# Four of the tiles that TensorE transposes go by DMA transfers of their own

## The chip, the cores and the metric

The kernel runs on one core of one Trainium2 chip. The metric is the time of one execution on the device in microseconds (us); the median of the runs is compared. TensorE multiplies matrices into PSUM, VectorE and ScalarE work element by element, GpSimd (POOL) does small things, and SyncE issues most DMA transfers, in order, from one queue.

## The reference

One block of a transformer with adaptive layer normalization. x has 2048 rows of 640; there are 32 heads of 128, with keys and values given (2048 each). In short:

```python
mod = (_silu(c) @ w_mod).reshape(c.shape[0], 6, 1, -1)
h = _layernorm(x, axis=-1) * (1 + ca) + sa
q = (h @ wq) per head
scores = jnp.einsum('bhqd,bhkd->bhqk', q, k_cache) * Dh ** (-0.5)
p = _softmax(scores, axis=-1)
o = jnp.einsum('bhqk,bhkd->bhqd', p, v_cache)
x = x + ga * (o @ wo)
h = _layernorm(x, axis=-1) * (1 + cb) + sb
x = x + gb * _B_ref(h, B_w1, B_w2, B_w3, B_w4)
```

`_B_ref` is a mixer with shifted rows and an MLP of width 1728. The change touches attention alone: the scores of 128 queries of one head against 2048 keys become exponentials, and these have to be turned (keys on the partitions) before they can be multiplied by V.

## The kernel before

**Tiles and steps.** A tile is 128 queries of one head: 16 tiles a head, 512 in all (NG), numbered through. The main loop (L684) takes one tile a step. In step s:

- TensorE makes the scores of tile s into the four banks of Sps, in two halves (`qk`, L352; its instructions stand at L359 and L15). Behind each half it multiplies half of the turned exponentials of tile s - 10 by V (`pv`, L365 and L373; PVD = 10). Then come pieces of the next head's Q (`q_piece`, L301) or a quarter of a transpose (below).
- VectorE reads each half of the scores, writes it scaled and negated to negS, and gathers the minimum of each row (L723). negS has three buffers, so tile s waits for the exponential of tile s - 3.
- POOL joins the two minima (L728). ScalarE takes the exponential into one place of `ring` (L731), 128 x 2048 bf16. It also copies the results of P V out of PSUM (L708), Q (L308), and TensorE's transposes (L333).

**Turning the exponentials.** `ring` has 20 places. Of 32 tiles (a pair of heads) 27 are turned by DMA, in trios of neighbouring tiles: when the last of the three has its exponential, SyncE issues one transfer from three neighbouring places to three others (`transpose`, L284, L286). The other five (tiles 3, 10, 17, 24 and 31 of the pair, the table PE_T) are turned by TensorE: eight f32 transposes of 128 x 128 (two bf16 keys taken as one f32), in four quarters spread over the half steps of two steps (`t_piece`, L319, L326), starting at the step that the table names (four steps after the tile, six for the last of the five). ScalarE copies the two halves back into the same place (`t_evac`, L330, L333). For such a tile VectorE writes even and odd keys apart (L720 to L722), and `pv` reads every second column (L372).

**Places.** The order of places is planned before the loop, L236 to L279. Trios use six windows of three places (WIN), tiles for TensorE the two single places 6 and 19 (ONE) in turn. PSL is the place that a tile's exponentials are written to, TSL that of the turned ones; `take` gives the place that has been free longest.

**Waits.** A recording layer (`Prog`) notes what each operation reads and writes, and puts a semaphore wait wherever another engine's or a transfer's work has to be over. All engines work in the order in which the loop records. SyncE's queue holds, besides the transposes, the loads of K (L222, by DMA transpose as well), of V (L231) and of wq (L226), one each for each head; K at the head's third step, V at its eleventh.

The pieces of Q are placed by `PIECES` (L335), in half steps that the table of TensorE's transposes leaves free. After the 512 tiles the output projection, the mixer and the MLP follow (from 1208 us).

Of the kernel before, what the change touches and what calls it, by code (L numbers as in the profile page):

```python
# [123 lines left out]
def bass_adaLN_cond__mha_block_cached__mixer_s_mlp__prompt_kernel(  # L124
# [21 lines left out]
    with ExitStack() as es:  # L146
# [9 lines left out]
        if True:  # L156
            with ExitStack() as es1:
# [4 lines left out]
                PE_AT = {32 * i + t: 32 * i + a for i in range(NG // 32) for t, a in PE_T.items()}  # L162
                PE_AT[NG - 2], PE_AT[NG - 1] = NG + 1, NG + 3
                del PE_AT[NG - 8]
                US = KT * (SQ + 4)
                small = sb1("small", [128, 4 * NQT + 32], F32)
                ring = sb1("ring", [128, NS, SK], BF16)
# [3 lines left out]
                mod_bc = sb1("mod_bc", [128, 4 * D], F32)  # L171
                hTx = sb1("hTx", [128, US], BF16)
                Of = sb1("Of", [128, 4, 2, 130], F32)
# [50 lines left out]
                def load_wq(h):  # L224
                    hb = h % 2
                    G.dma("sync", lambda e: e.dma_start(wq[:, hb], A_wq[:, h * 128:(h + 1) * 128].rearrange("(k p) d -> p k d", p=128)),  # L226
                          ("wq", hb), w=[("wq", hb)])
# [6 lines left out]
                is_pe = lambda g: g in PE_AT  # L234

                WIN = [0, 3, 7, 10, 13, 16]  # L236
                ONE = [6, 19]
                PSL, TSL, first_of, last_of = {}, {}, {}, {}
                free_at = dict(zip(WIN, (0, 2, 108, 1, 105, 106)))
                free_at.update(zip(ONE, (0, 1)))  # L240

                def take(opts):
                    a = min((a for a in opts if free_at[a] is not None), key=lambda a: free_at[a])
                    free_at[a] = None
                    return a
                todo = []
                for g in range(NG):
                    if is_pe(g):
                        PSL[g] = TSL[g] = g
                    else:  # L250
                        todo.append(g)
                trios = []
                while todo:
# [6 lines left out]
                for s in range(NG):  # L260
                    end = s >= NG - 10
                    g = s - PVD
                    if g in PSL and is_pe(g):
                        free_at[TSL[g]] = 100 + s
                    elif g in last_of:
                        free_at[TSL[last_of[g][0]]] = 100 + s + 1
                    if is_pe(s):
                        PSL[s] = TSL[s] = take(ONE)
                    if s in first_of:
                        m = first_of[s]  # L270
                        a = take([13] if m is trios[-1] else WIN[0:3] if end else WIN)
                        for i, g in enumerate(m):
                            PSL[g] = a + i
                    if s in last_of:
                        m = last_of[s]
                        a = take([7] if m is trios[-1] else WIN[3:6] if end else WIN)
                        for i, g in enumerate(m):
                            TSL[g] = a + i
                        free_at[PSL[m[0]]] = 100 + s + 6.5  # L279
# [4 lines left out]
                def transpose(m):  # L284
                    a, b, n = PSL[m[0]], TSL[m[0]], len(m)
                    G.dma("sync", lambda e: e.dma_start_transpose(  # L286
                        PTs[:, b:b + n].rearrange("p r k q -> p (r k) q"), ring[:, a:a + n].rearrange("p r s -> p (r s)")),
                        ("t", b), r=[k for i in range(n) for k in slot(a + i)], w=[k for i in range(n) for k in slot(b + i)])
# [395 lines left out]
                for s in range(NG + PVD + LAG):  # L684
                    h, j = divmod(s, NQT)
                    g_ = s - PVD
                    evacs = []
                    for half in range(2):
                        if s == 1:
                            spin_j(4 - half)  # L690
                        if s < NG:
                            qk(s, half)
                        if 0 <= g_ < NG:
                            pv(g_, half)
                        if h + 1 < H and 2 * s + half in PIECES[h]:
                            cc, q = PIECES[h][2 * s + half]
                            q_piece(h + 1, cc, q)
                            if q == KT - 1:
                                evacs.append((q_evac, h + 1, cc))
                        for g, r in t_of(s):  # L700
                            t_piece(g, r, half)
                            if half == 1:
                                evacs.append((t_evac, g, r))
                        for fn, *args in TAIL.get((s, half), ()):
                            fn(*args)
                    if 0 <= g_ < NG and g_ % 2 == 1:
                        p = g_ // 2
                        G.op("scalar", lambda a, p=p: a.copy(  # L708
                            Of[:, p % 4].rearrange("p z d -> p (z d)")[:, 0:259], PO[:, (p % 2) * 512:(p % 2) * 512 + 259]),
                            r=[("O", p % 2)], w=[("Of", p % 4)])  # L710
                    for fn, x, y in evacs:
                        fn(x, y)
                    for fn, *args in EARLY.get(s, ()):
                        fn(*args)
                    for half in range(2):
                        if s < NG:
                            r8 = s % 8
                            dst = negS[:, s % 3, half * 1024:(half + 1) * 1024]
                            src = Sps[:, half * 1024:(half + 1) * 1024]
                            if is_pe(s):  # L720
                                dst = dst.rearrange("p (b i z) -> p b z i", b=4, z=2)
                                src = src.rearrange("p (b z i) -> p b z i", b=4, z=2)  # L722
                            G.op("vector", lambda v, half=half, dst=dst, src=src, r8=r8: v.tensor_scalar(  # L723
                                out=dst, in0=src, scalar1=-SCALE, scalar2=None, op0=ALU.mult, op1=ALU.min,
                                accum_out=(nm0 if half == 0 else nm1)[:, r8:r8 + 1]),
                                r=[("S", half)], w=[("negS", s % 3), ("nmh", half, r8)])
                    if s < NG:
                        G.op("gpsimd", lambda g, r8=r8: g.tensor_scalar(  # L728
                            out=nm[:, r8:r8 + 1], in0=nm0[:, r8:r8 + 1], scalar1=nm1[:, r8:r8 + 1], scalar2=None, op0=ALU.min),
                            r=[("nmh", 0, r8), ("nmh", 1, r8)], w=[("nm", r8)])  # L730
                        G.op("scalar", lambda a, s=s, r8=r8: a.activation(  # L731
                            ring[:, PSL[s], :], negS[:, s % 3, :], ACT.Exp, bias=nm[:, r8:r8 + 1], scale=-1.0),
                            r=[("negS", s % 3), ("nm", r8)], w=slot(PSL[s]))
                        for fn, *args in LATE.get(s, ()):
                            fn(*args)
                        if s == OTS[0]:
                            ot0(0)
                        if s == 9 and H > 1:
                            load_k(1)
                            if H > 2:  # L740
                                load_wq(2)
                        if s in last_of:
                            transpose(last_of[s])
                        if j == 2 and h >= 1 and h + 1 < H:
                            load_k(h + 1)
                        if s in OTS[1:]:
                            ot0(OTS.index(s, 1))
                        if h and j == (0, 3)[h % 2] and h + 2 < H:
                            load_wq(h + 2)
                        if j == PVD and h + 1 < H:  # L750
                            load_v(h + 1)
                    if 0 <= s - PVD - LAG:
                        gr, z = divmod(s - PVD - LAG, 4)
                        if z == 0:
                            rcp(gr)
                        norm(gr, z)
                    if s == NG + PVD - 9:
                        G.op("gpsimd", lambda g: g.memset(mhalf, -0.5), w=["mhalf"] + NEG)
                        ot0(3)
                        load_ot(1, 0, H // 2, 0)  # L760
                        load_ot(1, H // 2, H, 1)
                        load_xt(0, 1)
# [281 lines left out]
```

## Time and profile before

| | |
|---|---|
| median of three runs | 1525.32 us (1523.91 to 1526.04) |
| the profiled execution | 1523.88 us, span 1522.0 us |
| attention, first to last VectorE instruction of L723 | 19.1 to 1207.6 us |
| transposes by DMA (L286) | 144, median 6.48 us in SyncE's queue, 9.6 us to landing |
| K loads (L222) | 32, median 2.3 us in the queue, 5.1 us to landing |
| copies of TensorE's transposes (L333) | 160 |
| TensorE's granted clock | 0.999 |

In the rows of groups the first number after the bar is busy time, then the mean length of one instruction in ns, then the engine's idle time before them and what ended it. Neighbouring instructions of VectorE and of ScalarE overlap in the records (the next begins before the last has ended), so the distance of two starts, not the length, is what an instruction costs. A SyncE row starts when the transfer's waits are over and ends when the queue goes on to the next entry; the landing comes later.

### The profile page before, as it was taken

The page shows a single profiled execution, that of the slowest core. Times are in us where ns is not written, and L with a number is a line of the kernel's source. Part 1 is how long each engine was busy: PE and PEld are TensorE (multiplying, and loading weights), DVE is VectorE, ACT ScalarE, POOL GpSimd, SP SyncE. Part 2 cuts the span into 40 slices and gives each one's busy share as a digit, 9 for nine tenths or more (in the row PEclk, how much of TensorE's full clock was granted, in tenths as well). Part 3 has the DMA queues.
Part 4 walks back from the last instruction along what each step waited for, and adds up shares of the span by engine and source line. Part 5 has one row for each costly group of instructions (what it writes and reads, how often), then busy time and mean ns, then how long its engine had stood idle before and what let it go on. Part 6 is the DMA issues. An engine that isn't in the chain of part 4 may idle for free.

```text
span 1522.0 us, 32831 instructions
## 1 busy us (share of the span) xinstructions
PE 1495.4 (98%) x13757; PEld 922.7 (61%) x12733; DVE 1369.4 (90%) x2424; ACT 1256.8 (83%) x1182; POOL 629.1 (41%) x1404
## 2 busy tenths in 40 slices
PE   8999999999999999999999999999999999999999
PEld 4566666656666666666666666666666665554545
DVE  8999999999999999999999999999999746767425
ACT  6999999999999999999999999999999700034230
POOL 1244444444444444444444444444444433333100
PEclk9999999999999999999999999999999999999999
DMA  9999999999999999999999999999999999734101
GB/s 325 254 244 247 251 229 255 234 229 249 243 229 254 243 243 232 242 244 241 240 236 241 245 233 247 243 234 246 246 240 229 242 222 215 152 83 108 35 22 35
DMA packets 1155297, 330.30 MB, mean 217 GB/s; under 512 B 1133322, under 2 KB 1149770, under 8 KB 1155146
## 3 DMA queue, kind: packets, MB, share of 16 engines
q1 hardware_dynamic: 1146656, 307.09, 100.5%
q0 software_dynamic: 6144, 16.79, 3.4%
q10 hardware_dynamic: 2346, 4.34, 0.8%
q8 instruction: 104, 1.70, 0.5%
q14 instruction: 47, 0.39, 0.1%
HBM read 43.48 MB, written 19.40 MB: 41 GB/s over the span
## 4 chain that ended last, share of the span: by engine, by line
ACT 73%; PE 18%; DVE 4%; DMA 2%; SPq 1%; issue 1%; POOL 0%; DVEq 0%; POOLq 0%
ACT ring L731 60%; PE Sps L654 7%; ACT ring L333 5%; ACT Of L708 4%; ACT kv L308 4%; PE Sps L981 4%; DVE negS L723 3%; PE Oaug L932 2%; PE QPp L932 2%; PE Sps L917 1%; DMA ring<-ring 1%; SPq L622 1%; SPq L286 1%; DMA ring<-in_A_x_dram 1%; ACT hTx L487 1%
## 5 line engine op out<-in xcount | busy, mean ns | idle before, releaser
L723 DVE TENSOR_SCALAR_CACHE_REDUCE negS<-Sps 128x1024 f32<-128x1024 f32 x1024 | 1174.6, 1225 | 5.8 <-PE Sps L15 3.0
L731 ACT ACTIVATE ring<-negS,small 128x2048 bf16<-128x2048 f32 x512 | 1115.5, 2403 | 1.6 <-POOL small L728 1.1
L373 PEld LDWEIGHTS PTp<-kv,ring 128*128 128x128 bf16 x8192 | 557.9, 98 | 302.7 <-issue 86.9
L373 PE MATMUL PTp<-kv,ring 128*128 128x129 bf16 x8192 | 645.1, 220 | 5.5 <-DMA ring<-ring 5.1
L359 PE MATMUL Sps<-kv 128*128 128x512 bf16 x1024 | 394.4, 385 | 8.1 <-DVE negS L723 4.5
L728 POOL TENSOR_SCALAR small<-small 128x1 f32<-128x1 f32 x512 | 146.1, 285 | 597.0 <-DVE negS L723 596.9
L15 PE MATMUL Sps<-kv 128*128 128x512 bf16 x1024 | 387.9, 379 | 0.0
L708 ACT COPY Of<-PTp 128x259 f32<-128x259 f32 x256 | 194.6, 760 | 3.9 <-PE PTp L373 3.9
L573 POOL TENSOR_SCALAR On<-Of,small 128x128 bf16<-128x128 f32 x512 | 189.8, 371 | 13.0
L359 PEld LDWEIGHTS Sps<-kv 128*128 128x128 bf16 x1024 | 98.2, 96 | 124.1 <-DVE negS L723 82.7
L566 POOL TENSOR_TENSOR small<-Of,small 128x4 f32<-128x4 f32 x128 | 133.1, 1040 | 13.7 <-ACT Of L708 13.4
L301 PE MATMUL QPp<-hTx,kv 128*128 128x512 bf16 x325 | 121.2, 378 | 1.1 <-ACT kv L308 1.1
L301 PE MATMUL Oaug<-hTx,kv 128*128 128x512 bf16 x315 | 118.5, 378 | 3.0 <-ACT kv L308 1.3
L580 POOL DMA_DIRECT2D o_scratch<-On x128 | 103.8, 811 | 40.8 <-POOL On L573 37.2
L723 DVE DVE_READ_ACCUMULATOR negS<-Sps 128x1 f32 x1024 | 90.5, 88 | 0.0
L855 ACT ACT_TABLE_LOAD x1 | 1.3, 1283 | 105.3 <-POOL hTx L873 105.3
L333 ACT COPY ring<-Oaug 128x512 f32<-128x512 f32 x78 | 76.6, 982 | 0.0
L333 ACT COPY ring<-QPp 128x512 f32<-128x512 f32 x77 | 76.3, 992 | 0.0
L767 POOL TENSOR_SCALAR negS<-negS 128x1 f32<-128x1 f32 x48 | 24.4, 509 | 116.8 <-DVE negS L776 116.8
L654 PE MATMUL Sps<-wo,negS 128*128 128x128 bf16 (+1 forms) x512 | 71.5, 299 | 0.4 <-DVE ring L782 0.4
L985 DVE TENSOR_TENSOR ring<-Sps,ring 128x640 f32<-128x640 f32 x15 | 12.4, 825 | 60.8 <-PE Sps L981 60.8
L308 ACT CAST kv<-QPp 128x512 bf16<-128x512 f32 x65 | 62.2, 956 | 1.3 <-PE QPp L301 1.3
(118 smaller groups left out, 1091.6 us busy)
## 6 DMA issues: line engine op xcount, KB each, us to landing
kv<-in_A_v_cache_dram SPq DMA_DIRECT2D x32, 512.0 KB, 5.3
o_scratch<-On POOLq DMA_DIRECT2D x128, 128.0 KB, 5.0
ring<-in_A_x_dram SPq DMA_DIRECT2D x8, 640.0 KB, 4.9
kv<-in_A_wq_dram SPq DMA_DIRECT2D x32, 160.0 KB, 3.6
wo<-in_A_wo_dram SPq DMA_DIRECT2D x1, 5120.0 KB, 21.6
ring<-in_w_mod_dram SPq DMA_DIRECT2D x5, 640.0 KB, 8.6
out_dram<-wo SPq DMA_DIRECT2D x15, 160.0 KB, 1.8
ring<-ring SPq DMA_TRANSPOSE x144, 9.6
```

Of the source, the lines that this page charges most:

```text
L15: return t.add_instruction(mybir.InstMatmult(name=t.bass.get_next_instruction_name(), ins=[t.lower_ap(rhs), t.lower_ap(lhsT)], outs=[t.low ...
L301: G.op("tensor", lambda t: t.matmul(JB[jb], wq[:, hb, q, :], hT[:, q, cc * 512:(cc + 1) * 512], start=(q == 0), stop=(q == KT - 1)), r=[(" ...
L333: G.op("scalar", lambda a: a.copy(dst, src), r=keys[-1:], w=[("PT", TSL[g], r)])
L359: ins = (t.matmul if c2 == 0 else partial(same_weights, t))(Sps[:, col:col + 512], QT[:, hb, j * 128:(j + 1) * 128], KTs[:, hb, col:col + ...
L373: ins = t.matmul(ob[:, 0:129], pt, Vaug[:, hb, kt, 0:129], start=(kt == 0), stop=(kt == NKT - 1))
L566: G.op("gpsimd", lambda g: g.tensor_tensor(out=rl[:, 4 * b:4 * b + 4], in0=Of[:].rearrange("p a z d -> p (a z) d")[:, 4 * b:4 * b + 4, 128 ...
L573: G.op("gpsimd", lambda g: g.tensor_scalar(out=On[:, b, z, :], in0=Of[:, 2 * b + z // 2, z % 2, 0:128], scalar1=rl[:, 4 * b + z:4 * b + z ...
L654: ins = t.matmul(YB[b][:, c0:c0 + cw], OTj[pr % 2][:, 2 * hh + z, :], wo[:, hh, c0:c0 + cw], start=(hh == 0), stop=(hh == H - 1))
L708: G.op("scalar", lambda a, p=p: a.copy(Of[:, p % 4].rearrange("p z d -> p (z d)")[:, 0:259], PO[:, (p % 2) * 512:(p % 2) * 512 + 259]), r= ...
L723: G.op("vector", lambda v, half=half, dst=dst, src=src, r8=r8: v.tensor_scalar(out=dst, in0=src, scalar1=-SCALE, scalar2=None, op0=ALU.mul ...
L728: G.op("gpsimd", lambda g, r8=r8: g.tensor_scalar(out=nm[:, r8:r8 + 1], in0=nm0[:, r8:r8 + 1], scalar1=nm1[:, r8:r8 + 1], scalar2=None, op ...
L731: G.op("scalar", lambda a, s=s, r8=r8: a.activation(ring[:, PSL[s], :], negS[:, s % 3, :], ACT.Exp, bias=nm[:, r8:r8 + 1], scale=-1.0), r= ...
```

## The change

In the second, sixth, tenth and fourteenth pair of heads the second of the five tiles (tiles 42, 170, 298 and 426, the list LONE) is no longer turned by TensorE. Its exponentials go to a single place as before; three steps later SyncE issues a transfer of this tile alone to the other single place, ahead of the trio that ends in the same step. The source's place is given back to the plan at that step, the target's when P V of the tile is over. VectorE and `pv` treat the tile like one of a trio, because `is_pe` is false for it. The four quarters on TensorE and the two copies on ScalarE fall away for it. `PIECES` is still made from the table (the tiles are taken out of PE_AT ahead of it, and the pieces of Q stand in the same half steps as before).

```diff
                 del PE_AT[NG - 8]
+                LONE = [32 * i + 10 for i in (1, 5, 9, 13)]
+                for g in LONE:
+                    del PE_AT[g]
...
                     if is_pe(g):
                         PSL[g] = TSL[g] = g
-                    else:
+                    elif g not in LONE:
                         todo.append(g)
...
                     g = s - PVD
-                    if g in PSL and is_pe(g):
+                    if g in PSL and (is_pe(g) or g in LONE):
                         free_at[TSL[g]] = 100 + s
                     elif g in last_of:
                         free_at[TSL[last_of[g][0]]] = 100 + s + 1
-                    if is_pe(s):
+                    if is_pe(s) or s in LONE:
                         PSL[s] = TSL[s] = take(ONE)
+                    if s - 3 in LONE:
+                        TSL[s - 3] = take(ONE)
+                        free_at[PSL[s - 3]] = 100 + s
...
+                        if s - 3 in LONE:
+                            transpose([s - 3])
                         if s in last_of:
                             transpose(last_of[s])
```

## The prediction

> **What bounds the kernel now.** I read the page first, then the list of waits, then VectorE and ScalarE in order of time, last SyncE's queue at the four places that the change touches. In the page:
>
> ```profile
> PE 1495.4 (98%) x13757; PEld 922.7 (61%) x12733; DVE 1369.4 (90%) x2424; ACT 1256.8 (83%) x1182; POOL 629.1 (41%) x1404
> ACT 73%; PE 18%; DVE 4%; DMA 2%; SPq 1%; issue 1%; POOL 0%; DVEq 0%; POOLq 0%
> L723 DVE TENSOR_SCALAR_CACHE_REDUCE negS<-Sps 128x1024 f32<-128x1024 f32 x1024 | 1174.6, 1225 | 5.8 <-PE Sps L15 3.0
> L731 ACT ACTIVATE ring<-negS,small 128x2048 bf16<-128x2048 f32 x512 | 1115.5, 2403 | 1.6 <-POOL small L728 1.1
> ```
>
> The attention stage (19 to 1208 us) holds the change. TensorE looks fullest, but is not the limit: its weight loads wait 82.7 us in all for VectorE (L723), while VectorE is idle only 5.8 us before L723. VectorE's 1,024 halves follow each other in 1.145 us, so 32 tiles (a pair of heads) need 64 x 1.145 = 73.28 us. ScalarE is idle even less, and the chain of waits runs through it (73%). So two engines are full at almost the same rate. Where they meet, around tile 255 (VectorE, then ScalarE in order of time, then the chain of waits in order of time):
>
> ```profile
> 616.48 1.22 DVE L723 TENSOR_SCALAR_CACHE_REDUCE negS<-Sps 128x1024 f32<-128x1024 f32 x1
> 618.21 1.23 DVE L723 TENSOR_SCALAR_CACHE_REDUCE negS<-Sps 128x1024 f32<-128x1024 f32 x1 [0.50 <-ACT ring L731]
> ```
>
> ```profile
> 615.06 4.56 ACT L731 ACTIVATE ring<-negS,small 128x2048 bf16<-128x2048 f32 x2
> 618.86 1.03 ACT L708 COPY Of<-PTp 128x259 f32<-128x259 f32 x1
> ```
>
> ```profile
> 606.26 3.79 ACT ring L731 x2
> 610.05 0.26 ACT Of L708
> 610.32 0.49 ACT kv L308
> 612.71 0.47 ACT ring L333
> 615.35 0.49 ACT ring L333
> ```
>
> VectorE starts 1.73 us after its last start instead of 1.145: it waits for an exponential of three tiles earlier, since negS has three buffers. ScalarE's cost by those rows, for 32 tiles: 32 exponentials x 1.895 + 16 copies of O x 0.26 + 8 of Q and 10 of transposed halves x 0.48 = 60.6 + 4.2 + 8.6 = 73.4 us, 0.16 more than VectorE needs. I went through the starts of all L723 instructions and added what exceeds 1.145 us. After a tile with ScalarE as releaser, or with ScalarE as the last one busy: tiles 127, 241, 255, 273, 280, 287, 305, 319, 337, 351, 383, 433, 447, 465, 479 and 497 give 0.27, 0.11, 0.58, 0.16, 0.02, 0.21, 0.16, 0.23, 0.15, 0.23, 0.58, 0.14, 0.23, 0.16, 0.23 and 0.16: 3.6 us. After one with TensorE late: 0.35, 1.15 and 0.41 (tiles 21, 28, 38), 1.17 (134), 0.15 (358), 0.07 (387) and 0.4 at the end: 3.7 us. Nothing else holds this stage up after tile 20, so a lighter ScalarE can give back at most 3.6 us.
>
> **The change, part by part.** For tiles 42, 170, 298 and 426:
>
> *Taken from ScalarE*: two copies (L333) a tile, 0.47 + 0.49 = 0.96 us, 3.8 us in all, at the 4th and 5th step after the tile. This lies on the path wherever ScalarE is the one behind. Over four pairs ScalarE runs 4 x 0.16 = 0.64 us over VectorE's time; one removal of 0.96 us covers that. Not all can be banked: the exponentials of tiles 288 to 319 start 1.1 to 2.2 us after VectorE's end of the same tile, and the least such distance anywhere is 0.42 us, so a lead of at least 1.1 - 0.4 = 0.7 us is won there, enough for four pairs. In the other three places the distance is partly at its least already (0.42 us in tiles 128 to 191), and some is lost. Bounds: all 3.6 us, or only the waits in the 22 tiles after tiles 298 and 426 (0.16 + 0.23 + 0.14 + 0.23 = 0.8 us). I take 3.1: 0.16 a pair says that the balance itself turns, which is nearer to the upper end; 0.5 us stays at local peaks.
>
> *Taken from TensorE*: 8 f32 transposes a tile with their loads (L326, 273 ns each, overlapped; the half steps that hold them last 1.13 us in TensorE's order). It isn't late there, so 0; the place in the order stays empty, since the pieces of Q stay where they were.
>
> *VectorE and POOL*: the tile's minimum is written without the even-odd split. Medians are 1.221 us with the split and 1.220 us without: 0. POOL: nothing moves. P V of the tile reads plain columns instead of every second one: same shape, 0.
>
> *Added to SyncE's queue*: one transfer (L286's function) a tile of 128 x 2048, three steps after the tile, after V's load and ahead of the trio that ends in that step. It has to wait for the exponential, three steps old, and for P V of the tile seven before, whose place it writes. The queue at the four places (SyncE in order of time):
>
> ```profile
> 135.90 0.58 SPq L231 DMA_DIRECT2D kv<-in_A_v_cache_dram  x1
> 138.27 7.32 SPq L286 DMA_TRANSPOSE ring<-ring  x1
> 430.95 0.58 SPq L231 DMA_DIRECT2D kv<-in_A_v_cache_dram  x1
> 433.15 6.36 SPq L286 DMA_TRANSPOSE ring<-ring  x1
> 725.03 0.58 SPq L231 DMA_DIRECT2D kv<-in_A_v_cache_dram  x1
> 728.09 6.15 SPq L286 DMA_TRANSPOSE ring<-ring  x1
> 1019.63 0.58 SPq L231 DMA_DIRECT2D kv<-in_A_v_cache_dram  x1
> 1022.68 6.72 SPq L286 DMA_TRANSPOSE ring<-ring  x1
> ```
>
> Free time between V's issue and the trio: 1.8, 1.6, 2.5, 2.5 us. P V of tiles 35, 163, 291 and 419 ended at 134.3, 428.7, 722.8 and 1017.5 us, before V's issue: the new wait holds nobody. Price of the transfer in the queue: a third of a trio (median 6.48 / 3 = 2.2 us), or a K transpose of the same 512 KB (median 2.3, least 1.7). So the trio behind it starts 0.4 to 0.7 us late twice, not at all twice. Those trios land 2.3, 2.5, 3.7 and 2.6 us before TensorE reads them: hidden. In the next four issues the queue again waits for ScalarE, so the delay doesn't add up. If that cover were gone, the next late thing is TensorE's wait for the trios with least reserve, those of tiles 185 to 190 (0.74 and 0.05 us) and 309 to 315 (0.98 and 0.56 us).
>
> The Trainium skill ("DMA: Bandwidth & Descriptors", section "Anatomy of one DMA") speaks against a transfer of its own: a fixed 2 us or so for each, plus bytes over 436 GB/s. As an estimate from that page 512 KB would be 3.2 us; the sum would still be 3.1 us of gain, since even with all 3.2 us in the queue the trio behind would be 0.7 to 1.6 us late, less than its reserve. The K rows (2.3 us in the queue, 5.1 to landing) agree with a fixed part that lies in the landing, where that section puts most of it.
>
> The tile itself would land about 5 us after issue (K's median), so at 141.5 us for tile 42; P V reads it at 148.5, and tile 49's exponential writes the source's place at 145.3. Both covered, by 7 and 4 us. The two single places 6 and 19 change roles after each such tile; no other order moves.
>
> Sum against the profiled execution: 1523.88 - 3.1 = 1520.8 us (its span 1522.0 and 1.9 around it). That execution lies 1.4 below the median of the runs shown, 1525.32, from which I subtract the same: 1522.2 us. Their spread is 2.1 us; 0.2%, 3.05 us, is about what a measurement can tell from no change here.
>
> **The rivals.**
>
> *Only local relief.* If ScalarE's lead isn't banked (it reaches its least distance and idles), only 0.8 to 2.6 us come back: about 1523.6 us. For it: 0.42 us of distance in tiles 160 to 191, around the second place. Against: from tile 256 on VectorE loses 0.39 us in every pair (73.64 us for 73.25), so ScalarE is behind all the time there.
>
> *The wait changes hands.* TensorE's weight loads for P V already wait 16 times for a trio (12.8 us). When VectorE stops waiting at tiles 127, 255 and 383, late trios of tiles 117 to 126 and 373 to 382 (reserve 0.05 us) may stop it instead: 1.2 us of the gain goes, and with leftover peaks about nothing stays: 1525 us. Against: TensorE needs 1.115 to 1.13 us a half, so it gains on VectorE between such places.
>
> *Slower: the transfer costs as a trio.* If issue were mostly a price per transfer, 6.3 us instead of 2.2, the trio behind would start 4 to 5 us late, past its reserve of 2.3 to 3.7 and TensorE's lead of about 0.7; that trio and the next two (reserve 0.5 to 1.8) would stop VectorE for some 1.7 us each time: 4 x 1.7 = 6.8 for 3.1 won, 1529 us. It decides from about 5 us in the queue (free 2, reserve 2.5, lead 0.7). For it: K issues of 512 KB are not all short, 3.15 us at 225 us and 7.7 at most. Against: their median of 2.3 us in the same queue.
>
> **How the numbers follow.** Balance turns, 1522.2 us (its own range 1521 to 1523.3): 0.50, of which 0.43 below 1522.27. Local relief: 0.27, of which 0.03 below it. Wait changes hands: 0.10, all within 0.2%. Slower: 0.13. That makes 0.46 faster, 0.41 the same, 0.13 slower. Range: from 1520.3 (all 3.6 us, and the spread of a median) to 1526.5 (the third case and its spread); the slower case is left out, and a little below.
>
> **What would show it.** ACT-released gaps of VectorE's L723 nearly gone after tile 127; 64 halves in 73.3 us instead of 73.64 for tiles 256 to 351; 8 copies of L333 fewer; four transfers more of L286's kind, about 2.2 us in the queue each; no new wait of L373 for DMA within 20 us behind them. Wrong if TensorE's waits for trios grow by more than 3 us, or if VectorE's gaps behind tiles 273 to 351 stay as they are.

## The result, and the profile after

The changed kernel is slower: 1528.19 us median (1524.08 to 1532.09, 22 runs) against 1525.61 us (1523.64 to 1528.95, 22 runs); the ratio is 1.0017, with a 95% interval of 1.0011 to 1.0023. That is a loss of 2.6 us where 3.1 us of gain were forecast, outside the stated range. The runs also spread more: 8 us instead of 5.3.

The profiled execution took 1528.83 us, with a span of 1527.0; it differs from the profiled one of before by 5.0 us, about twice what the medians differ by. Its page:

```profile
ACT 58%; PE 18%; DVE 13%; DMA 5%; issue 4%; SPq 1%; POOL 0%; DVEq 0%; POOLq 0%
L729 DVE TENSOR_SCALAR_CACHE_REDUCE negS<-Sps 128x1024 f32<-128x1024 f32 x1024 | 1173.9, 1222 | 9.9 <-PE Sps L15 8.8
L737 ACT ACTIVATE ring<-negS,small 128x2048 bf16<-128x2048 f32 x512 | 1073.9, 2193 | 4.6 <-POOL small L734 4.3
```

ScalarE's share of the chain fell from 73% to 58%, and it now waits 4.3 us for its input (1.1 before). That alone doesn't show the relief: with the transfer and no relief (below) it waits 4.6 us as well. VectorE stands idle 9.9 us ahead of L729 (5.8 before), 8.8 of it for TensorE. Why TensorE is late, in the lists of waits of the kernel before (first two lines) and of the changed kernel (total, times, longest):

```profile
PEld PTp L373 <- DMA ring<-ring: 12.8, 16, 1.9
DVE negS L723 <- PE Sps L15: 3.0, 5, 1.1
...
PEld PTp L379 <- DMA ring<-ring: 22.8, 26, 2.9
PE PTp L379 <- DMA ring<-ring: 10.1, 12, 2.4
DVE negS L729 <- PE Sps L15: 8.8, 10, 2.2
```

With the starts of all L729 instructions added up as in the prediction, VectorE's gaps after tile 20 are now:

| VectorE's gaps, us | behind ScalarE | behind TensorE | sum |
|---|---|---|---|
| before | 3.6 | 3.7 | 7.3 |
| changed kernel | 1.2 | 9.9 | 11.1 |

The difference, 3.8 us, is about that of the lengths of this stretch, 3.7 us. (The whole stages differ by 3.3 us and the spans by 5.0; the rest is VectorE's first wait of the next stage, for rows of x, 30.8 us instead of 29.1.) The largest new gap, VectorE in order of time at tile 195, without the rows of its DVE_READ_ACCUMULATOR:

```profile
477.05 1.22 DVE L729 TENSOR_SCALAR_CACHE_REDUCE negS<-Sps 128x1024 f32<-128x1024 f32 x1
480.51 1.23 DVE L729 TENSOR_SCALAR_CACHE_REDUCE negS<-Sps 128x1024 f32<-128x1024 f32 x1 [2.24 <-PE Sps L15]
482.66 1.22 DVE L729 TENSOR_SCALAR_CACHE_REDUCE negS<-Sps 128x1024 f32<-128x1024 f32 x1 [0.91 <-PE Sps L15]
```

And what TensorE waited for there, in order of time:

```profile
479.03 0.64 PE L379 MATMUL PTp<-kv,ring 128*128 128x129 bf16 x8 [2.38 <-DMA ring<-ring]
...
480.27 1.07 PE L379 MATMUL PTp<-kv,ring 128*128 128x129 bf16 x8
```

This is the trio of tiles 185 to 187, which the prediction named as one of those with least reserve. The wait costs more than itself: behind it eight such matmuls take 1.07 us instead of 0.64, because TensorE's granted clock is 0.63 from 480.5 to 484.5 us (1.00 in the 3.5 us after that). VectorE's next two gaps, 1.00 and 0.41 us, are waits for this slower TensorE. Whether every wait of that length brings this on isn't shown. SyncE's queue at the first and the third of the four places:

```profile
128.75 6.77 SPq L292 DMA_TRANSPOSE ring<-ring  x1
135.56 0.59 SPq L234 DMA_DIRECT2D kv<-in_A_v_cache_dram  x1
136.25 4.04 SPq L292 DMA_TRANSPOSE ring<-ring  x1
140.39 6.53 SPq L292 DMA_TRANSPOSE ring<-ring  x1
...
727.36 0.58 SPq L234 DMA_DIRECT2D kv<-in_A_v_cache_dram  x1
728.04 3.83 SPq L292 DMA_TRANSPOSE ring<-ring  x1
```

The single transfer holds the queue 4.04, 4.33, 3.83 and 3.94 us, not 2.2, and the trio behind it (140.39) starts 2.9 us after its exponential was ready. The table shows by how much each of the next eight trios starts late (start in the queue less the end of the exponential that it needs, mean of the four places), and the reserve that is left (TensorE's first read less landing; 0.05 means that TensorE stood waiting; means of four places as well).

| trio behind the place | 1st | 2nd | 3rd | 4th | 5th | 6th | 7th | 8th |
|---|---|---|---|---|---|---|---|---|
| late, before | 0.03 | 0.15 | 0.70 | 0.73 | 0.02 | 0.49 | 0.13 | 0.02 |
| late, changed | 2.28 | 2.81 | 3.37 | 3.09 | 1.22 | 3.71 | 2.14 | 1.10 |
| reserve, before | 2.78 | 2.47 | 1.99 | 1.17 | 1.23 | 1.17 | 3.13 | 3.25 |
| reserve, changed | 0.05 | 0.55 | 0.57 | 0.49 | 0.32 | 0.93 | 1.86 | 1.90 |

The lateness isn't taken up by the next pause of the queue. It lasts about eight trios, 25 tiles or 57 us, and for six of them less than 1 us of reserve is left in the mean. The fifth trio shows how a pause goes: in the kernel before the queue waited ahead of it, behind the next load of V; now it follows V's load at once and lasts 9.3 us instead of 7.1, and the sixth is later than the first.

### The profile page after: what moved, and what is told of

Its sections match the earlier page's. It is cut to its first block, busy times and chain, and to the rows that moved or that the text cites. A ratio compares the mean times of both kernels' runs of the same rounds, so it can differ in the third digit from the quotient of the medians.

```text
span 1527.0 us, 32771 instructions
## 1 busy us (share of the span) xinstructions
PE 1494.1 (98%) x13725; PEld 919.4 (60%) x12701; DVE 1368.6 (90%) x2424; ACT 1255.3 (82%) x1174; POOL 629.0 (41%) x1404
## 4 chain that ended last, share of the span: by engine, by line
ACT 58%; PE 18%; DVE 13%; DMA 5%; issue 4%; SPq 1%; POOL 0%; DVEq 0%; POOLq 0%
ACT ring L737 47%; DVE negS L729 12%; PE Sps L660 7%; PE Sps L989 4%; ACT ring L339 4%; ACT Of L714 3%; ACT kv L314 3%; DMA ring<-ring 3%; PE Oaug L940 2%; PE QPp L940 2%; PE Sps L925 1%; DMA ring<-in_A_x_dram 1%; SPq L628 1%; SPq L292 1%; ACT hTx L493 1%
## 5 line engine op out<-in xcount | busy, mean ns | idle before, releaser
L729 DVE TENSOR_SCALAR_CACHE_REDUCE negS<-Sps 128x1024 f32<-128x1024 f32 x1024 | 1173.9, 1222 | 9.9 <-PE Sps L15 8.8
L737 ACT ACTIVATE ring<-negS,small 128x2048 bf16<-128x2048 f32 x512 | 1073.9, 2193 | 4.6 <-POOL small L734 4.3
L714 ACT COPY Of<-PTp 128x259 f32<-128x259 f32 x256 | 140.8, 550 | 5.7 <-PE PTp L379 5.7
L729 DVE DVE_READ_ACCUMULATOR negS<-Sps 128x1 f32 x1024 | 87.9, 86 | 0.0
L660 PE MATMUL Sps<-wo,hTx 128*128 128x512 bf16 (+1 forms) x448 | 61.8, 299 | 0.0
L660 PEld LDWEIGHTS Sps<-wo,negS 128*128 128x128 bf16 x512 | 40.1, 98 | 34.3 <-DVE ring L790 1.7
L332 PE MATMUL Oaug<-identf,ring 128*128 128x128 f32 x296 | 57.1, 274 | 0.0
```

The costliest lines, as they stand in the source:

```text
L660: ins = t.matmul(YB[b][:, c0:c0 + cw], OTj[pr % 2][:, 2 * hh + z, :], wo[:, hh, c0:c0 + cw], start=(hh == 0), stop=(hh == H - 1))
L714: G.op("scalar", lambda a, p=p: a.copy(Of[:, p % 4].rearrange("p z d -> p (z d)")[:, 0:259], PO[:, (p % 2) * 512:(p % 2) * 512 + 259]), r= ...
L737: G.op("scalar", lambda a, s=s, r8=r8: a.activation(ring[:, PSL[s], :], negS[:, s % 3, :], ACT.Exp, bias=nm[:, r8:r8 + 1], scale=-1.0), r= ...
```

## The experiments

Ratios are to the kernel before, run beside. Theory A: the relief is worth what was forecast, and the transfer in the queue takes it back. Theory B: the relief is worth nothing, because a VectorE that ScalarE doesn't stop is stopped by late trios anyway.

### The two halves of the change, each alone

The relief alone: the four tiles stay in their place unturned.

```diff
-                    if s - 3 in LONE:
-                        TSL[s - 3] = take(ONE)
-                        free_at[PSL[s - 3]] = 100 + s
...
-                        if s - 3 in LONE:
-                            transpose([s - 3])
```

> The four tiles are turned by nobody: TensorE's transposes and ScalarE's two copies of them fall away, and no transfer takes their place (P V reads the four tiles unturned, so that part of the computation is left out). Theory A (ScalarE's relief is worth what was forecast, and the loss comes from the transfer in SyncE's queue): faster than before by 2 to 3.6 us, VectorE's gaps behind ScalarE after tile 128 fall from 3.3 to under 1.5 us, TensorE's waits for trios stay at the 13 us of before. Theory B (relief is worth nothing: a VectorE that isn't stopped by ScalarE is stopped by late trios instead): within 1 us of before, TensorE's waits for trios grow by 2 us or more.

Measured: 1523.21 us, ratio 0.9983 (0.9973 to 0.9992), 2.6 us faster. Gaps behind ScalarE 1.6 us, behind TensorE 3.9. TensorE's waits are those of before:

```profile
PEld PTp L376 <- DMA ring<-ring: 13.0, 16, 1.7
```

The transfer alone, added to the kernel before:

```diff
+                        if s - 3 in LONE:
+                            b_ = TSL[s - 10]
+                            G.dma("sync", lambda e, b_=b_: e.dma_start_transpose(
+                                PTs[:, b_:b_ + 1].rearrange("p r k q -> p (r k) q"), wof[:, 0:SK]),
+                                ("t", b_), r=["wo"], w=slot(b_))
```

> TensorE and ScalarE turn the four tiles as before, and at the place of the changed kernel's four transfers SyncE issues a transfer of the same size into the same single place, from wo (its data is overwritten unused). Theory A: slower than before by 4 to 7 us, since the loss of 2.6 us and the relief of 2 to 3.6 us add up; the transfer holds the queue about 4 us, the trio behind starts 1.5 to 3 us late, and VectorE's gaps behind TensorE grow by 4 us or more. Theory B: slower by about as much as the changed kernel, 2.6 us.

Measured: 1528.57 us, ratio 1.0015 (1.0007 to 1.0024). This run's list of waits:

```profile
PEld PTp L374 <- DMA ring<-ring: 29.3, 32, 2.4
DVE negS L724 <- PE Sps L15: 8.4, 14, 1.6
```

The transfer held the queue 4.1 to 5.0 us and its trio started 2.65 us late, as theory A said; but the time is that of the changed kernel, as theory B said. The two do not add: 0.9983 and 1.0015 would make 0.9998, and the change makes 1.0017. The gaps tell why. With the transfer alone, those behind ScalarE are already down to 1.7 us (3.6 before), while those behind TensorE are 10.3: while TensorE holds VectorE up, ScalarE catches up. So most of the fall from 3.6 to 1.2 us in the changed kernel isn't the relief's; on top of the transfer the relief takes 1.7 to 1.2.

### What makes the transfer take 4 us

V's load stands right ahead of the single transfer. First, V's load moved behind the trio that follows:

```diff
-                        if j == PVD and h + 1 < H:
+                        if j == (13 if 16 * h + 10 in LONE else PVD) and h + 1 < H:
                             load_v(h + 1)
```

> The changed kernel, with V's load in the four heads moved from the step two before... three steps ahead of the single transfer to the place behind the trio that follows it. Theory C (the transfer holds the queue 4 us and not 2.2 because it stands right behind V's load and has to wait until V's 512 KB are through; the free time seen in the queue before was V's): the single transfer takes 2.0 to 2.5 us in the queue, the trio behind it starts less than 0.7 us late, and the time falls to 1523 to 1526 us. Theory D (a transfer of its own costs about 4 us wherever it stands): 3.8 us or more in the queue, and a time like the changed kernel's, 1527 to 1529 us.

Measured: 1529.53 us, ratio 1.0019 (1.0008 to 1.0030). The queue at the third place:

```profile
728.65 1.66 SPq L292 DMA_TRANSPOSE ring<-ring  x1
```

1.86, 2.22, 1.66 and 2.35 us at the four places: theory C is right about the transfer, and its forecast of the time is wrong. The trio behind it starts 0.25 us late, but the next three, behind V's load, 1.5, 3.9 and 3.7 us: the work is only moved. The trio that now follows V's load directly lasts 8.2 us instead of 6.8. Second, V's load left out in the four heads:

```diff
-                        if j == PVD and h + 1 < H:
+                        if j == PVD and h + 1 < H and 16 * h + 10 not in LONE:
                             load_v(h + 1)
```

> The changed kernel without V's load in the four heads ahead of whose single transfer it stands (four of the 32 loads are left out, so those heads multiply by an older V). Theory C (V's 512 KB and the single transfer together are more than the queue's free time there; the rest of the pair works it off): the single transfer takes about 2.2 us in the queue, the trio behind it starts on time, no lateness is passed on, and the time is that of the relief alone, 1522 to 1524.5 us. If a single transfer costs the pair something else than its place in the queue (its two waits, its places): still 1526 us or more.

Measured: 1525.69 us, ratio 0.9996 (0.9987 to 1.0004); 2.2 to 2.4 us in the queue, and the first, second and fifth trio behind on time within 0.7 us (the third and fourth 2.0 and 1.6 us late, with the relief alone 1.8 and 1.3). The loss is gone, but the time is 2 us above that of the relief alone.

The landings tell what the transfer waits for. In the changed kernel its entry in the queue ends 0.18 to 0.28 us before V's load lands, at all four places (at 140.29 for 140.50 us at the first), and 0.15 to 0.23 us before with the transfer alone. In these two runs without V directly ahead, its 1.7 to 2.4 us end between 0.2 us before and 0.7 us behind the landing of the trio ahead. So how long a transfer of this size holds the queue follows what ahead of it is still under way.

The same as the last run without the transfer, so relief and four V loads fewer:

> The relief alone (nobody turns the four tiles, P V reads them unturned), and V's load left out in the same four heads as in the run without V: that run less the four single transfers. If a single transfer that has room in the queue costs nothing: the same time as that run, within 1 us of 1525.7 us, or 1523 like the relief alone. If the transfer still costs something although its followers start on time: 1521 to 1523 us, 2 us or more below it.

Measured: 1526.72 us, ratio 0.9998 (0.9989 to 1.0008), the same as with the transfer. So a transfer that has V's room in the queue costs nothing that shows. Why these two don't show the gain of the relief stays open; in this run's profile, taken in one of its longest executions, 4.7 of 8.7 us of gaps behind TensorE lie at tiles 21 to 29, ahead of anything that was changed.

Then the size, half of it (256 KB) in the run of the transfer alone:

```diff
-                                PTs[:, b_:b_ + 1].rearrange("p r k q -> p (r k) q"), wof[:, 0:SK]),
+                                PTs[:, b_, 0:NKT // 2, :], wof[:, 0:SK // 2]),
```

> The transfer alone, at half its size (256 KB from wo, into half of the same place; TensorE and ScalarE turn the four tiles as before). Theory C (the loss grows with the time by which transfer and V exceed the queue's free time of 1.6 to 2.5 us): about 3 us in the queue instead of 4.1, the trio behind starts 1 to 2 us late instead of 2.65, and the time is 0.5 to 2 us above before instead of 2.9. A price for each transfer: 2.5 to 3 us above before, as with the whole size.

Measured: 1524.97 us, ratio 1.0001 (0.9992 to 1.0009). The queue at the first place:

```profile
136.78 0.58 SPq L232 DMA_DIRECT2D kv<-in_A_v_cache_dram  x1
137.47 3.24 SPq L745 DMA_TRANSPOSE ring<-wo  x1
```

2.75 to 3.5 us, ending 1.0 to 1.5 us before V's load lands; the trio behind 1.4 us late, and the next ones 1.1, 1.9, 1.5 and 0.1. So half a transfer costs nothing that shows, and the whole, with its trio 2.65 us late, 2.3 us. Theory C is right about the queue and a little too high in the time; a price for each transfer is ruled out. That the loss begins where the lateness exceeds the reserve fits both sizes, but two sizes don't show the point.

### How many, and where

Fourteen pairs instead of four (`for i in range(1, 15)`):

> The changed kernel with a single transfer in each of the pairs 1 to 14 and not in four. Theory A: each costs the queue about 4 us, which dies out only over a whole pair of heads, so the queue never catches up: slower than before by 10 to 25 us, TensorE's waits for trios over 60 us. Theory B (the loss is a matter of four places): slower by 3.5 times 2.6, about 9 us. If ScalarE's relief were all that counts: faster by 3 us.

Measured: 1548.43 us (1536.03 to 1549.84), ratio 1.0125 (1.0094 to 1.0157). Some 1.4 us a place, twice the 0.65 of four places. The profiled execution doesn't say why: it was the one short one, 1536.03 us or 0.75 us a place, the other three took 1547 to 1550. In it TensorE's weight loads waited 49.8 us for trios (over 60 were expected), and the last trio ahead of the next place was only 0.4 us late in the mean, so that there the lateness hardly added up. The three longer ones had a lower granted clock (0.994 to 0.996, against 0.998); what they lost their time on isn't shown. The fourth tile of the five instead of the second (`32 * i + 24`):

> The changed kernel with the fourth tile of the five (24 of the pair) by the single transfer instead of the second. By theory C and the reserve of the trios behind it: V's load stands right ahead there too, the free time is about 1 us instead of 1.6 to 2.5 and the trios that follow have 0.5 to 2 us of reserve instead of 2.3 to 3.7, but the next pair's first trios, with more reserve, work it off sooner: between 1527 and 1532 us. If the place doesn't matter: 1528 us.

Measured: 1528.30 us, ratio 1.0013 (1.0002 to 1.0024). The transfer held the queue 3.8 to 5.2 us behind V's load there. The place makes no difference that can be told.

### Is the relief real?

Four runs side by side. The relief in fourteen pairs, only ScalarE's copies left out, work added to ScalarE, and the relief of four once more. The edits of the second and third:

```diff
-                            if half == 1:
+                            if half == 1 and g not in (42, 170, 298, 426):
                                 evacs.append((t_evac, g, r))
```

```diff
+                def t_more(g, r):
+                    for k in range(7):
+                        i = 4 + 28 * r + 4 * k
+                        G.op("scalar", lambda a, i=i: a.copy(small[:, i:i + 4], mod_bc[:, 0:4]), r=["mod"], w=[("more", r, k)])
...
                                 evacs.append((t_evac, g, r))
+                                if 40 < g < 480 and g % 32 == 10:
+                                    evacs.append((t_more, g, r))
```

> Relief alone in the pairs 1 to 14 instead of four (14 tiles are turned by nobody, P V reads them unturned): 13.4 us less work for ScalarE. If ScalarE's gaps are what the relief gives back, the gain stops at the 3.6 us that they sum to before: 2 to 4 us faster, gaps behind ScalarE under 0.5 us. If the relief is worth nothing, because TensorE's waits for trios take the gaps' place: within 1 us of before.

> Only ScalarE's two copies of the four tiles are left out (TensorE still transposes them, P V reads them unturned). If the gain of the relief is ScalarE's: the same as the relief alone beside it, 1.5 to 3.5 us faster than before. If it is TensorE's, which gets free half steps and so more lead over late trios: within 0.7 us of before.

> The kernel before with 14 small copies (128 x 4, into unused columns) added on ScalarE behind the second tile of 14 pairs, 196 in all. By the rows of L333 and L708 (512 columns in 0.48 us, 259 in 0.26) one costs ScalarE 0.04 us by extrapolation, so 0.55 us a tile and 8 us in all. If ScalarE is the limit beside VectorE: slower by 4 to 10 us. If it has slack that the gaps don't show: within 1 us.

> The relief alone in the four pairs, as in the first study, beside the three others. If the relief is worth what the first run gave: 1.5 to 3.5 us faster than before. If that run was luck: within 1 us of before.

| run | ratio | gaps behind ScalarE | behind TensorE |
|---|---|---|---|
| relief in 14 pairs | 0.9960 (0.9947 to 0.9972) | 0.3 | 0.8 |
| copies only, 4 tiles | 0.9980 (0.9971 to 0.9989) | 2.5 | 2.9 |
| ScalarE's extra copies | 1.0128 (1.0113 to 1.0144) | 23.2 | 1.7 |
| relief, 4 tiles | 0.9985 (0.9976 to 0.9993) | 2.0 | 1.3 |

The gaps are those of one profiled execution each. The relief is worth 2.3 us (0.15%) here, 2.6 in the first run, and it is ScalarE's: without its copies alone, with all of TensorE's transposes, 3.0 us come back. In fourteen pairs it is 6.1 us, more than the 4 expected: the gaps behind TensorE go as well (3.7 to 0.8), with TensorE's waits for trios down to 4.5 us. The extra copies give the sharpest reading. The chain of waits in order of time at the first of them:

```profile
138.31 0.47 ACT ring L333
138.78 0.66 ACT small L338 x7
139.44 1.90 ACT ring L738
141.34 0.26 ACT Of L715
141.60 0.49 ACT ring L333
142.09 0.65 ACT small L338 x7
```

Seven copies take 0.65 to 0.66 us, so 28 times that, 18.4 us, were added, and the kernel is 19.5 us slower (1.28%). ScalarE has no slack in this stage that would hide them; VectorE waits for it (1.2 us in 3 waits before):

```profile
DVE negS L730 <- ACT ring L738: 18.3, 30, 0.9
```

(One copy cost 0.094 us, not the 0.04 extrapolated from two lengths, so the expected total was too low.)

### Two ways to make room

All of V's loads but the first issued by POOL, with the change and without:

```diff
-                    G.dma("sync", lambda e: e.dma_start(Vaug[:, hb, :, 0:128], ...
+                    G.dma("gpsimd" if h else "sync", lambda e: e.dma_start(Vaug[:, hb, :, 0:128], ...
```

> The changed kernel with all of V's loads but the first issued by POOL, so that they stand in another queue than the transposes. Theory Q (the limit is the order in SyncE's one queue): the single transfer takes 2 to 2.5 us, the trios start on time, and the time falls to 1522 to 1525 us. Theory E (the limit is the 16 DMA engines that both queues share): V's bytes slow the transposes just as much, the issues behind the single transfer are late by 2 us or more as before, and the time stays at 1527 to 1530 us.

> The kernel before with the same move of V's loads to POOL. Theory Q: TensorE's waits for trios fall and the time by 1 to 2 us, to about 1524 us. Theory E: within 1 us of before.

Measured: ratios 1.0378 (1.0354 to 1.0403) and 1.0343 (1.0315 to 1.0371), so 52 us lost for the kernel before, against both theories. Its list of waits:

```profile
PEld PTp L373 <- DMA ring<-ring: 65.9, 34, 6.4
DVE negS L723 <- PE Sps L15: 52.0, 38, 6.2
```

TensorE waits up to 6.4 us for a trio. V's loads themselves land after 8.0 us instead of 5.3. The trios that are under way when POOL issues V, those that end in tiles 9 and 23 of a pair, land 13.1 and 13.2 us after their start instead of 8.8 and 9.9 (medians), and their reserve falls from 3.1 and 1.4 us to 0.05. Then the opposite, the writes to o_scratch issued by SyncE too, so that all traffic of the stage stands in one queue:

```diff
-                    G.dma("gpsimd", lambda e: e.dma_start(
+                    G.dma("sync", lambda e: e.dma_start(
                         o_scr[jj // 2:jj // 2 + 2, :, hh].rearrange("a p z d -> p a (z d)"),
```

> The kernel before with the 128 writes of attention's output to o_scratch issued by SyncE instead of POOL, so that all traffic of the stage stands in one queue. V's loads in POOL's queue cost 51 us, so traffic of another queue seems to hold up the transposes beyond its bytes. Theory S (that holds for o_scratch too): trios take about 6.0 us in the queue instead of 6.5, TensorE's waits for trios fall below 8 us, the time falls by 1 to 3 us. Theory T (SyncE's queue is the scarce thing, and 128 issues of 0.6 us, with waits for POOL, fill it further): slower by 5 us or more.

> The changed kernel with the same move of o_scratch's writes to SyncE. Theory S: the single transfers find room, the loss of 2.6 us turns into the gain of the relief, 1520 to 1523.5 us. Theory T: slower than the changed kernel by 5 us or more, since the queue works off no lateness.

Measured: 1.0028 (1.0017 to 1.0039) and 1.0087 (1.0070 to 1.0105). Theory T is right: in sign for the kernel before, 4.3 us where 5 or more were expected, and in size for the changed one, 10.7 us above the changed kernel. On top of the move the change costs about 9 us instead of 2.6. A fuller queue makes the same four transfers dearer.

### Both together, with half transfers

Since half a transfer stays hidden, the last two runs turn the first half of the keys of the tile by a transfer and the second half by TensorE, with one copy of ScalarE:

```diff
-                            pt = PTr[:, b, kt // 2, :, kt % 2] if is_pe(g) else PTs[:, b, kt, :]
+                            pt = PTr[:, b, kt // 2, :, kt % 2] if is_pe(g) or (g in LONE and half == 1) else PTs[:, b, kt, :]
...
-                    return [(g, s - a) for g, a in PE_AT.items() if a <= s < a + 2]
+                    return [(g, s - a) for g, a in PE_AT.items() if a <= s < a + 2] + [(g, 1) for g in LONE if s == g + 5]
...
-                            transpose([s - 3])
+                            transpose_half(s - 3)
```

> A full kernel: in seven pairs (1, 3, ... 13) the first half of the second tile's keys goes by a transfer of 256 KB at the changed kernel's place, the second half by TensorE and one copy of ScalarE as before. Relief 7 x 0.48 = 3.4 us instead of 3.8, each transfer about 3 us in the queue instead of 4. If the half transfer stays within the reserve of the trios: 1 to 3 us faster than before. If lateness adds up as with whole transfers: 1 us slower or more.

> The same in 14 pairs (1 to 14): relief 6.7 us, of which at most the 6 us of the relief in 14 pairs can come back. If the half transfers stay hidden: 3 to 5 us faster than before. If they don't (the queue has to work off 1 to 2 us in every pair): between 1 us faster and 5 us slower.

Measured: 1.0006 (0.9995 to 1.0016) and 1.0001 (0.9989 to 1.0014). In the two profiled executions the gaps behind ScalarE fall to 0.4 and 0.0 us, and those behind TensorE rise to 4.8 and 5.5, so that the sums, 5.2 and 5.5, lie under the 7.3 of before. But these two, 1522.55 and 1521.52 us, are among the shortest of their runs; over all runs nothing is left of it, and neither of the two expected cases came. No version that computes the reference was found to be faster than the kernel before.

## Why the prediction was wrong

*ScalarE as the second full engine, and what its relief is worth*: right. 3.1 us were forecast, 2.3 to 3.0 are measured for it alone, and 18.4 us of added work cost 19.5. (One run, the relief with four loads of V fewer, shows no gain; that stays open.) The gaps behind ScalarE, forecast to be nearly gone, fell less: the relief alone leaves 1.6 and 2.0 us of 3.6. The 1.2 us of the changed kernel don't bear the forecast out, since the transfer alone leaves 1.7.

*The price of the transfer in the queue*: wrong, 2.2 us forecast, 3.8 to 4.3 measured. A third of a trio is what it costs without V directly ahead of it (1.7 to 2.4 us). The step that failed is the reading of "free time between V's issue and the trio", 1.6 to 2.5 us. The queue was free because SyncE had nothing to issue, but V's load was only issued, not landed: with the transfer directly behind it, SyncE stands until V's load is nearly through (0.2 to 0.3 us before it lands). What SyncE lacks until then isn't shown. The profile before had the sign of this: trios that start less than 0.4 us behind V's load last 7.8 to 9.3 us in the queue (three), those 0.9 to 1.3 us behind 7.2 to 9.1 (five), and those more than 1.5 us behind it 6.4 in the median (23).

*"The delay doesn't add up"*: wrong, and the dearer mistake. It was argued from the next four issues, which wait for ScalarE on time in the kernel before. A queue that is late has no such waits left: in the 73.3 us of a pair, seven trios at 6.4 us, two directly behind V at 8.9, two K at 2.3 and four short loads at 0.6 take 69.6 us (medians of the changed kernel and of the kernel before), so that it makes up about 0.4 us a trio, as an estimate. A lateness of 2.3 us lasted eight trios, through those with 1.2 us of reserve in the mean. The prediction's own sign of being wrong came with it: TensorE's waits for trios grew by 10.0 us, where 3 were the limit.

*The reserve of the first trio*: 2.3 to 3.7 us, forecast to hide the delay. It did hide a delay of 1.4 us on the whole (the half transfer; TensorE stood waiting at one of the four places), and was used up by 2.3.

*The fixed price of about 2 us* that the Trainium skill gives ("DMA: Bandwidth & Descriptors", section "Anatomy of one DMA", which writes of transfers that GpSimd issues; these are SyncE's): the runs don't show one in the queue. Without V directly ahead the whole transfer took 1.7 to 2.4 us there, less than the sum of 3.2, and behind V half of it took about 1 us less than the whole.

*The rivals*: the slower one named the right chain (single transfer, late trio, TensorE, VectorE) and, by luck, nearly the time, 1529 us: its reason, a price for each transfer, is wrong, and it put the point from which it decides at 5 us in the queue; 4 were enough. One reason is TensorE's lead, put at 0.7 us: in the kernel before, the last matmul of a half ends 0.4 us ahead of VectorE's start on it (median), and the wait of 2.38 us above cost VectorE 2.32. "The wait changes hands" is not what happened: with the relief alone TensorE waits for trios as before (13.0 us), and the late trios of the changed kernel are late because of the transfer.

*The sum*: the loss was put at nothing, and in the slower rival gain and loss were taken as terms that add. They overlap: VectorE's stop for one engine is time in which the other catches up, so the change (1.0017) came out like its bad half alone (1.0015).

## What to carry to other kernels

A pause in an issuing queue need not be free time: look at whether the transfer ahead has landed, and at how long the next one takes to issue. What a delay in a queue costs is read from how fast the queue recovers (here 0.4 us a trio) and from the smallest reserve among all transfers until then, not from the reserve of the first one. Where two engines are both full, moving work from one to a third resource paid here only while that third had reserve of its own, and the two effects did not add.

## What the runs showed that was not expected

V's 31 loads in POOL's queue beside the transposes cost 52 us, 1.7 us each, while in SyncE's own queue they fit between the trios. POOL also spends 1.2 us on each issue, and ScalarE waits 25.5 us for POOL (1.1 before). But the trios under way at V's issue, which land 3.3 to 4.3 us later than before, say that the transposes themselves were held up; the first of the two starts on time (0.03 us late). Some of the loss is TensorE's clock: at eight of these waits the granted clock was half for 3.4 to 6.8 us (0.50 from 711.7 to 718.3 us, 0.988 over the run), and behind each of VectorE's three longest gaps (3.7, 4.3 and 6.3 us) another of 1.0 us follows. What the DMA engines do with the two queues isn't shown by these runs. The Trainium skill ("DMA: Bandwidth & Descriptors", section "Queues, rings and completion order") says that each DMA engine takes turns between its queues, packet by packet. The longer landings of V and of the trios under way agree with that, but it gives no reason for a loss beyond the bytes.

A half transfer of 256 KB four times costs nothing that shows, a whole one 2.3 us: the step lies between 1.4 and 2.65 us of lateness at the first trio. The least reserve in the mean (1.2 us) plus TensorE's lead of 0.4 us lies between them; that this is the measure isn't shown.
